# Tying each query output sum to a place in TensorE's queue

## The chip, the cores and the metric

The kernel runs on one core of a Trainium2 chip. The metric is the device time of one execution, in microseconds (us). The kernel before has a median of 917.51 us over three runs (915.57 to 920.6).

## The reference, cut to what matters

Three stages follow one another. A linear attention (4 batches, 8 heads, 576 tokens, head size 64) maps q and k through `phi`; a gated MLP, called moe1 here, works on the 2304 tokens; a top-1 mixture of 8 experts, called moe2, works on its output.

```
phi(x): p = x @ w_phi; p -= max|p|; concat(exp(p), exp(-p))
kv = phi(k)^T @ v;  z = sum(phi(k))
attn = (phi(q) @ kv) / (phi(q) @ z + 1e-6)
moe1 = (silu(xn @ w_gate) * (xn @ w_val)) @ w_out      # xn = rmsnorm(attn)
moe2 = gate * (relu(moe1[e] @ w1[e]) @ w2[e])          # e = argmax of the logits
```

## The kernel before, in words

Matmuls take their operands as pairs of 16-bit parts (high and low), so most products are three matmuls.

**Attention of batch b.** `k_unit(h)` (L275 on) projects the keys of a head and takes their exponentials; `kv(h)` (L306 on) sums them with v. `q_unit(p, rp)` (L324 on) does the same for the queries of a pair of heads, `rp` being the first or second half of the 512 main tokens, and ends in a DMA transpose issued from SP (L365), which writes the tile eT. `oo(p, rp)` (L378 on) is the query output sum of the change: 24 matmuls of eT with kv (L387) into a tile of tag ko, and a division on VectorE (`divide`, L371 on: L374, L375, L376). `oo_tail(j)` (L400 on, matmuls at L411) is the same for the last 64 tokens, twice per batch. `norm` and `ntr` (L417 on) then scale the rows and transpose them by DMA (L435) into xT of a token group.

**moe1 of token group g** (256 tokens). `m1_mm` (L509 on, matmuls at L520) makes gate and value products from xT into the PSUM tile gv: 12 matmuls for each of the two, 24 for each of 12 columns c. `m1_act` makes hT from them, and `m1_out_mm` (L535 on, matmuls at L542) sums po, six steps of 12 per group. Group 2b holds the first half of batch b, 2b+1 the second half, group 8 all the tails.

**Order.** `_weave` calls the steps of a main list in turn and after each of them so many steps of a side list that both end together. Main list of batch b: first the 24 gv steps of group 2b, with the six po steps of group 2b-1 put in behind column 1, then the same for group 2b+1. Side list of the first: the query units and output sums of the second half of batch b, its tails, and 65% of the key steps of batch b+1. Side list of the second: the rest of the keys and the first half of the queries of batch b+1. In batch 0 keys and first-half queries come ahead of all moe1 products. So an output sum of the second half is written behind the first products of group 2b, which read the xT that the first half feeds.

The order written is a priority. The framework plans all engines in a simulated timeline and lets an instruction go ahead of others that are written earlier where those aren't ready yet in its plan; the resulting order per engine is fixed in the program, and on the chip each engine works through its queue in that order.

**Shared slots.** The tag ko has two PSUM slots, which kv, oo, the tails (oot) and the router's logits (lgp, L568) take in turn. The tag E4 has four SBUF slots for the exponentials of keys and queries and for two of three eT tiles. The sums of kv lie in eight buffers that the last reader, the tail, sets free for the next batch.

Of the kernel before, what the change touches and what calls it, by code (L numbers as in the profile page):

```python
# [62 lines left out]
def body(ctx, tc, k0, kt0, q0, qt0, kk, kkt, qq, qqt, vv, vvt, w_phi, w_gv, w_out, rms_g, mid, w_g2, mbias,  # L63
         w1, w2, consts, out):
    nc = tc.nc
    V, A, G, SP, PE = nc.vector, nc.scalar, nc.gpsimd, nc.sync, nc.tensor
# [71 lines left out]
    wo = mw.tile([128, 12, 2, DM], F16, name="wo")  # L138
# [62 lines left out]
    state = {}  # L201

    def xT_group(g):
        if g not in xT:
            if g == 8:
                xT[g] = mx.tile([128, 8, 256], F16, tag="xTt", bufs=1, name="xTt")
            else:
                xT[g] = mx.tile([128, 8, 256], F16, tag="xT", bufs=3, name=f"xT{g}")
        return xT[g]
# [7 lines left out]
    def attention(b, banks, eng, pp_lo):  # L217
# [4 lines left out]
        t, m, kvs, x = {}, {}, {}, {}  # L222
# [223 lines left out]
        def seq(*fs):  # L446
            def run():
                for f in fs:
                    f()
            return run  # L450

        def L(f, *a):
            return lambda: f(*a)


        ks = [begin, seq(L(prep, "k", 4), L(prep, "k", 0), L(load, "k", 1)), L(prep, "v", 4)]
        order = [8] + list(range(8))
        for n, h in enumerate(order + [None]):
            pre = []
            if h is not None and h < 8:  # L460
                p = h // 2
# [15 lines left out]
        def q_steps(rp):  # L477
            st = []
            for p in range(5):
                fs = []  # L480
                if p < 4:
                    fs.append(L(q_unit, p, rp))
                    if rp == 0:
                        if p + 1 < 4:
                            fs.append(L(prep, "q", p + 1))
                        if p + 2 < 4:
                            fs.append(L(load, "q", p + 2))
                    elif p == 0:
                        fs.append(L(load, "q", 4))
                    elif p == 1:  # L490
                        fs.append(L(prep, "q", 4))
                if p < 4:
                    st.append(seq(*fs))
                elif rp == 1:
                    st += [L(q_unit, 4, 0)]
                if p >= 2:
                    st.append(L(oo, p - 2, rp))
            if rp == 1:
                st.append(tail_m)
            st.append(L(oo, 3, rp))  # L500
            st += [seq(L(norm, 2 * rp)), seq(L(norm, 2 * rp + 1), L(ntr, 2 * rp)), L(ntr, 2 * rp + 1)]
            return st
        tail = [L(oo_tail, 0), L(oo_tail, 1), L(norm, 4), L(ntr, 4)]
        return ks, q_steps(0), q_steps(1), tail


    hT = {}

    def m1_mm(g, c, which):  # L509
        x = xT_group(g)  # L510
        if which == 0:
            hT[g, c] = None
            state["gv", g, c] = ps_gv.tile([128, 2, 256], F32, tag="gv", name="gv")
        p = state["gv", g, c]
        f = slice(128 * c, 128 * c + 128)
        w = wgv[which]
        n = 0
        for kc in range(4):
            for wl, xl in ((0, 0), (0, 1), (1, 0)):
                PE.matmul(p[:, which, :], lhsT=w[:, kc, wl, f], rhs=x[:, 4 * xl + kc, :],  # L520
                          start=(n == 0), stop=(n == 11))
                n += 1

    def m1_act(g, c):
# [10 lines left out]
    def m1_out_mm(g, i, third):  # L535
        if third == 0:
            state["o", g, i] = ps_o.tile([128, DM], F32, tag="po", name="po")
        p = state["o", g, i]
        tk = slice(128 * i, 128 * i + 128)
        for c in range(4 * third, 4 * third + 4):  # L540
            for hl, wl in ((0, 0), (0, 1), (1, 0)):
                PE.matmul(p, lhsT=hT[g, c][:, hl, tk], rhs=wo[:, c, wl, :],  # L542
                          start=(c == 0 and hl == 0 and wl == 0), stop=(c == 11 and hl == 1))

    def m1_evict(g, i):
        p = state.pop(("o", g, i))
# [27 lines left out]
    def out_steps(g):  # L574
        st = []
        for i in range(2):
            for th in range(3):
                def s(i=i, th=th):
                    m1_out_mm(g, i, th)
                    if th == 2:  # L580
                        m1_evict(g, i)
                    if th == 0 and i == 1:
                        m1_store(g, 0)
                st.append(s)
        return st

    def group_steps(g, prev):

        st = []
        for c in range(12):  # L590
            st.append(lambda c=c: m1_mm(g, c, 0))

            def s(c=c):
                m1_mm(g, c, 1)
                m1_act(g, c)
                if prev is not None:
                    if c == 2:
                        m1_store(prev, 1)
                    if c == 4:
                        m1_logits(prev, 0)  # L600
                    if c == 6:
                        m1_logits(prev, 1)
            st.append(s)
            if c == 1 and prev is not None:
                st += out_steps(prev)
        return st
# [441 lines left out]
    narrow = ((ps_pj, "pj"),)  # L1048
    bk = list(wide)
    att = [attention(b, bk if b == 0 else narrow, EXP_SPLIT[b].split(), PREP_LO[b]) for b in range(4)]  # L1050
    done = [0]

# [20 lines left out]
    for b in range(4):  # L1073
# [8 lines left out]
        n = KSPLIT * len(ks) // 100  # L1082
        s0, s1 = side + ks[:n], ks[n:] + att[b + 1][1]
        if b == 0:
            w = []
# [6 lines left out]
        n = len(wst) // 2  # L1092
# [7 lines left out]
    rp = ctx.enter_context(tc.tile_pool(name="rp", bufs=1, side="right", reuse_waits="tile"))  # L1100
# [6 lines left out]
    n = len(w2s) * M7 // (M7 + 12)  # L1107
# [103 lines left out]
```

## Time and profile before

| | |
|---|---|
| median of three runs | 917.51 us |
| profiled execution, its own time | 921.32 us |
| its span, first to last instruction | 919.5 us |
| TensorE busy | 810.0 us (88%) |
| VectorE busy | 593.0 us (64%) |
| ScalarE busy | 431.0 us (47%) |
| granted TensorE clock, mean | 0.94 |
| mean DMA rate | 215 GB/s |

A row of the timeline is: start, duration, engine, line, operation, out<-in, shape, count, and in brackets how long the engine stood idle before it and what ended that. A matmul's row overlaps the next by some 0.2 us, since matmuls are pipelined.

### The profile page before, as it was taken

The numbers are of one execution on the slowest core, as the hardware profiler recorded it, in microseconds if no ns is written. First come the engines' busy times: TensorE is split into PE (matmuls) and PEld (weight loads), VectorE is DVE, ScalarE is ACT, GpSimd is POOL, SyncE is SP. The second block draws the span as 40 slices with busy tenths as digits, with TensorE's granted clock in tenths as the row PEclk, the third lists the DMA queues.
The fourth block names the chain that finished last, engine by engine and source line by source line (L and its number), as shares of the span: only waits on it lengthen the run. The fifth ranks groups of instructions, "written<-read, shape, count | busy, mean of one in ns | idle before, by whom it ended". The sixth has DMA issues, their size and how long they took to land. (4 is left out here: it accounts for less than half of the span.)

```text
span 919.5 us, 18449 instructions
## 1 busy us (share of the span) xinstructions
PE 810.0 (88%) x6840; PEld 557.5 (61%) x6840; DVE 593.0 (64%) x1448; ACT 431.0 (47%) x1125; POOL 86.3 (9%) x104
## 2 busy tenths in 40 slices
PE   5744699998889988979998989998899998999995
PEld 4534588776577766666786667675674443444442
DVE  6989897897688877868988866356835311221121
ACT  4787555486656666757767744234321111111110
POOL 0001030000130000211000202000010222111010
PEclk8657689999989999999999999999999999999999
DMA  8579878589899799899879986897995599699732
GB/s 278 139 193 215 209 155 191 150 215 228 212 218 260 237 242 242 212 227 242 220 213 235 234 230 189 326 344 249 266 353 132 120 224 226 143 286 257 155 70 52
DMA packets 266590, 197.39 MB, mean 215 GB/s; under 512 B 212863, under 2 KB 214271, under 8 KB 262912
## 3 DMA queue, kind: packets, MB, share of 16 engines
q1 hardware_dynamic: 263296, 186.21, 78.9%
q0 software_dynamic: 3200, 9.97, 3.4%
q8 instruction: 55, 0.90, 0.4%
q14 instruction: 39, 0.32, 0.1%
HBM read 164.92 MB, written 43.52 MB: 227 GB/s over the span
## 5 line engine op out<-in xcount | busy, mean ns | idle before, releaser
L520 PEld LDWEIGHTS <-wgv 128*128 128x128 f16 x2592 | 256.9, 100 | 69.1 <-issue 21.9
L520 PE MATMUL gv<-xT,wgv 128*128 128x256 f16 x2304 | 280.0, 280 | 20.0 <-DVE hu L530 13.2
L542 PE MATMUL po<-wo,hT 128*128 128x512 f16 x648 | 151.6, 379 | 0.1
L635 ACT ACTIVATE w2b<-w2a 128x512 f16<-128x512 f32 x128 | 80.9, 632 | 115.1 <-DMA w2a<-in_w_dram 109.3
L636 DVE SCALAR_TENSOR_TENSOR w2b<-w2a,w2b 128x512 f16<-128x512 f32 x128 | 89.7, 701 | 65.4 <-ACT w2b L635 64.8
L994 PE MATMUL m2y<-L,hsT 128*128 128x512 f16 x480 | 106.7, 379 | 4.8 <-DMA hsT<-hs 4.8
L981 ACT ACTIVATE hs<-m2h 128x512 f16<-128x512 f32 x40 | 23.9, 597 | 181.4 <-PE m2h L978 179.4
L978 PE MATMUL m2h<-L,xT 128*128 128x512 f16 x480 | 107.0, 379 | 2.0 <-DMA L<-ws 1.8
L542 PEld LDWEIGHTS <-hT 128*128 128x128 f16 x648 | 61.1, 98 | 62.0 <-DVE hT L152 1.3
L994 PEld LDWEIGHTS <-hsT 128*128 128x128 f16 x480 | 46.7, 98 | 62.0 <-DMA hsT<-hs 6.3
L978 PEld LDWEIGHTS <-xT 128*128 128x128 f16 x480 | 46.6, 98 | 58.6 <-issue 2.5
L982 DVE SCALAR_TENSOR_TENSOR hs<-m2h,hs 128x512 f16<-128x512 f32 x40 | 27.6, 691 | 80.9 <-ACT hs L981 76.5
L423 POOL TENSOR_TENSOR x<-x,g_bc 128x512 f32<-128x512 f32 x16 | 21.9, 1368 | 483.0 <-ACT xg L422 482.4
L387 PE MATMUL oo<-kv,eT 128*128 128x65 f16 x768 | 32.4, 202 | 37.3 <-DMA eT<-eq 30.6
L151 ACT CAST hT<-hu 128x256 f16<-128x256 f32 x108 | 43.5, 405 | 30.2 <-DVE hu L530 28.7
L528 DVE SCALAR_TENSOR_TENSOR th<-th,gv 128x256 f32<-128x256 f32 x108 | 44.7, 414 | 20.1 <-ACT th L527 19.7
L358 ACT ACTIVATE e<-pj,b 128x128 f32<-128x128 f32 x144 | 54.6, 379 | 4.2 <-DVE eq L152 2.5
L387 PEld LDWEIGHTS <-eT 128*128 128x128 f16 x768 | 29.6, 103 | 43.7 <-DMA eT<-eq 36.0
L359 ACT ACTIVATE e<-pj,b 128x128 f32<-128x128 f32 x144 | 55.4, 385 | 0.0
L527 ACT ACTIVATE th<-gv 128x256 f32<-128x256 f32 x108 | 41.3, 382 | 30.1 <-PE gv L520 30.0
L152 DVE TENSOR_TENSOR eq<-e,eq 128x512 f16<-128x512 f32 x72 | 52.0, 726 | 3.7 <-ACT eq L151 3.4
L997 DVE TENSOR_SCALAR y<-m2y,iBg 128x512 f32<-128x512 f32 x16 | 12.0, 751 | 65.1 <-PE m2y L994 65.1
(226 smaller groups left out, 1095.5 us busy)
## 6 DMA issues: line engine op xcount, KB each, us to landing
L<-ws SPq DMA_DIRECT2D x88, 1024.0 KB
w2a<-in_w_dram SPq DMA_DIRECT2D x128, 256.0 KB
ws<-w2b SPq DMA_DIRECT2D x128, 256.0 KB
wst<-in_w_gv_dram SPq DMA_DIRECT2D x24, 512.0 KB
wst<-in_w_out_dram SPq DMA_DIRECT2D x12, 512.0 KB
xs<-x SPq DMA_DIRECT2D x18, 256.0 KB
v<-in_vv_dram SPq DMA_DIRECT2D x16, 260.0 KB
k<-in_kk_dram SPq DMA_DIRECT2D x12, 256.0 KB
```

Of the source, the lines that this page charges most:

```text
L151: A.copy(dst_hi, src)
L152: (V if lo == "v" else G).tensor_tensor(out=dst_lo, in0=src, in1=dst_hi, op=ALU.subtract)
L358: A.activation(out=e[:, r, 0, :], in_=pp[:, j, :], func=AF.Exp, scale=sc, bias=b1[:, j:j + 1])
L359: A.activation(out=e[:, r, 1, :], in_=pp[:, j, :], func=AF.Exp, scale=-sc, bias=b2[:, j:j + 1])
L387: PE.matmul(acc[:, j, :], lhsT=et[:, hl * 8 + j * 2 + s, :], rhs=kvs[2 * p + j % 2][:, vl, s, :], start=(n == 0), stop=(n == 5))
L520: PE.matmul(p[:, which, :], lhsT=w[:, kc, wl, f], rhs=x[:, 4 * xl + kc, :], start=(n == 0), stop=(n == 11))
L528: V.scalar_tensor_tensor(out=t, in0=t, scalar=1.0, in1=p[:, 0, :], op0=ALU.add, op1=ALU.mult)
L542: PE.matmul(p, lhsT=hT[g, c][:, hl, tk], rhs=wo[:, c, wl, :], start=(c == 0 and hl == 0 and wl == 0), stop=(c == 11 and hl == 1))
L635: A.activation(out=o[:, :, 0, :], in_=t, func=AF.Copy, scale=WS)
L636: V.scalar_tensor_tensor(out=o[:, :, 1, :], in0=t, scalar=WS, in1=o[:, :, 0, :], op0=ALU.mult, op1=ALU.subtract)
L978: PE.matmul(p, lhsT=x[:, 4 * xl + kc, :], rhs=w[:, kc, half, wl, :], start=(n == 0), stop=(n == 11))
L994: PE.matmul(p, lhsT=t[:, 4 * hl + i, :], rhs=w[:, fc, wl, :], start=(fc == 0 and hl == 0 and wl == 0), stop=(fc == 7 and hl == 1))
```

## The change

`late` wraps a call. When a moe1 product has been emitted already, everything that the call puts on TensorE gets an ordering edge to the product emitted last: its place in the queue must be behind that product. It is an edge of order alone, without a semaphore. All calls of `oo` and `oo_tail` are wrapped; `m1_mm` and `m1_out_mm` record their matmuls in `state["main"]`. The first four output sums of batch 0 are emitted ahead of every moe1 product and stay free.

```
+        def late(f, *a):
+            def run():
+                if "main" in state:
+                    with tc.issue_after(state["main"].ins):
+                        f(*a)
+                else:
+                    f(*a)
+            return run
...
                 if p >= 2:
-                    st.append(L(oo, p - 2, rp))
+                    st.append(late(oo, p - 2, rp))
             if rp == 1:
                 st.append(tail_m)
-            st.append(L(oo, 3, rp))
+            st.append(late(oo, 3, rp))
...
-        tail = [L(oo_tail, 0), L(oo_tail, 1), L(norm, 4), L(ntr, 4)]
+        tail = [late(oo_tail, 0), late(oo_tail, 1), L(norm, 4), L(ntr, 4)]
...
-                PE.matmul(p[:, which, :], lhsT=w[:, kc, wl, f], rhs=x[:, 4 * xl + kc, :],
+                state["main"] = PE.matmul(p[:, which, :], lhsT=w[:, kc, wl, f], rhs=x[:, 4 * xl + kc, :],
...
-                PE.matmul(p, lhsT=hT[g, c][:, hl, tk], rhs=wo[:, c, wl, :],
+                state["main"] = PE.matmul(p, lhsT=hT[g, c][:, hl, tk], rhs=wo[:, c, wl, :],
```

## Rows read from the trace of the kernel before

**Rows 1.** Busy time by stretch: window, length, engines (count), clock, DMA share, GB/s.

```profile
313.70:375.50 61.80, 54.93 (x578) 42.92 (x578) 45.92 (x113) 38.38 (x107) 0.00 (x0) 0.97 0.92 233
...
566.50:919.50 353.00, 328.04 (x1903) 179.18 (x1903) 125.06 (x369) 66.23 (x136) 42.11 (x43) 0.99 0.77 212
```

**Rows 2.** Waits of TensorE: total us, times, longest us.

```profile
PE oo L387 <- DMA eT<-eq: 30.6, 12, 6.9
...
PE gv L520 <- DMA xT<-xg: 6.6, 4, 4.5
PE oo L387 <- DVE x L376: 5.7, 3, 3.0
```

**Rows 3.** Timeline of TensorE, 60 to 150 us: the start of batch 0's products.

```profile
84.97 0.96 PE L387 MATMUL oo<-kv,eT 128*128 128x65 f16 x24 [2.62 <-DMA eT<-eq]
...
91.08 1.50 PE L387 MATMUL oo<-kv,eT 128*128 128x65 f16 x24 [2.96 <-DMA eT<-eq]
...
96.24 1.50 PE L387 MATMUL oo<-kv,eT 128*128 128x65 f16 x24 [0.87 <-DMA eT<-eq]
102.22 7.33 PE L520 MATMUL gv<-xT,wgv 128*128 128x256 f16 x48 [4.48 <-DMA xT<-xg]
109.38 0.90 PE L387 MATMUL oo<-kv,eT 128*128 128x65 f16 x24
...
123.10 2.78 PE L520 MATMUL gv<-xT,wgv 128*128 128x256 f16 x24 [1.66 <-DVE hu L530]
125.72 2.77 PE L318 MATMUL kv<-v,ek 128*128 128x65 f32 x20
```

**Rows 4.** Timeline of TensorE, 212 to 273 us: the change from group 1 to 2.

```profile
212.98 5.40 PE L520 MATMUL gv<-xT,wgv 128*128 128x256 f16 x48
...
222.32 0.45 PE L568 MATMUL lgp<-wg,x2T 128*128 128x8 f16 x12
222.63 0.89 PE L387 MATMUL oo<-kv,eT 128*128 128x65 f16 x24
...
235.69 0.89 PE L387 MATMUL oo<-kv,eT 128*128 128x65 f16 x24 [0.57 <-DVE x L376]
...
243.56 1.63 PE L387 MATMUL oo<-kv,eT 128*128 128x65 f16 x48
...
251.45 0.89 PE L387 MATMUL oo<-kv,eT 128*128 128x65 f16 x24 [2.99 <-DVE x L376]
255.10 1.53 PE L411 MATMUL oot<-kv,eT 128*64 128x65 f16 x24 [2.76 <-DMA eT<-eq]
257.02 6.74 PE L520 MATMUL gv<-xT,wgv 128*128 128x256 f16 x48 [0.39 <-DMA xT<-xg]
263.69 0.95 PE L411 MATMUL oot<-kv,eT 128*64 128x65 f16 x24
...
272.40 1.40 PE L318 MATMUL kv<-vs,ek 128*128 128x65 f16 x30
```

**Rows 5.** Timeline of SP's DMA issues, 170 to 265 us.

```profile
192.68 2.02 SPq L365 DMA_TRANSPOSE eT<-eq  x1
...
250.07 1.49 SPq L365 DMA_TRANSPOSE eT<-eq  x1
251.65 3.48 SPq L435 DMA_TRANSPOSE xT<-xg  x2
```

**Rows 6.** Timeline of VectorE, 232 to 266 us: the ends of divisions.

```profile
242.01 0.74 DVE L376 TENSOR_TENSOR x<-oo,ep 128x256 f32<-128x256 f32 x2
...
258.14 0.41 DVE L376 TENSOR_TENSOR x32t<-oot,ep 64x256 f32<-64x256 f32 x1
```

**Rows 7.** Timeline of TensorE in batches 2 and 3.

```profile
384.03 0.90 PE L387 MATMUL oo<-kv,eT 128*128 128x65 f16 x24
...
387.82 5.40 PE L520 MATMUL gv<-xT,wgv 128*128 128x256 f16 x48 [0.87 <-DMA xT<-xg]
...
545.45 0.34 PE L387 MATMUL oo<-kv,eT 128*128 128x65 f16 x6 [2.17 <-DVE x L376]
```

More of the change, by code (lines that the diff above doesn't have):

```diff
@@ L519, in m1_mm @@
             for wl, xl in ((0, 0), (0, 1), (1, 0)):
-                PE.matmul(p[:, which, :], lhsT=w[:, kc, wl, f], rhs=x[:, 4 * xl + kc, :],
-                          start=(n == 0), stop=(n == 11))
+                state["main"] = PE.matmul(p[:, which, :], lhsT=w[:, kc, wl, f], rhs=x[:, 4 * xl + kc, :],
+                                          start=(n == 0), stop=(n == 11))
                 n += 1
@@ L541, in m1_out_mm @@
             for hl, wl in ((0, 0), (0, 1), (1, 0)):
-                PE.matmul(p, lhsT=hT[g, c][:, hl, tk], rhs=wo[:, c, wl, :],
-                          start=(c == 0 and hl == 0 and wl == 0), stop=(c == 11 and hl == 1))
+                state["main"] = PE.matmul(p, lhsT=hT[g, c][:, hl, tk], rhs=wo[:, c, wl, :],
+                                          start=(c == 0 and hl == 0 and wl == 0), stop=(c == 11 and hl == 1))
     def m1_evict(g, i):
```

## The prediction, made before the result was known

> **What bounds the kernel now.** I read the busy time by stretch first. From 566.5 us to the end TensorE works 328 of 353 us [rows 1]: whatever the attention loses or wins before that arrives at the end one for one, unless a slack behind it takes it up. Ahead of that the rows show an engine that is nearly full but not quite: 54.9 of 61.8 us in the stretch of group 3 [rows 1]. So I ask what TensorE waits for there. The list of waits says that the largest single one is output sums waiting for the transposed exponentials, 30.6 us in 12 waits; next to it stand 6.6 us of moe1 waiting for its own transposed input, and 5.7 us of output sums waiting for a division to set a ko slot free [rows 2]. A change that moves output sums back in the queue seems made for the 30.6 us. Whether it is depends on what stands behind each waiting sum, so the third view is the timeline.
>
> It shows where second-half sums stand today. In batch 0 three of them run at 84.97, 91.08 and 96.24 us, and only at 102.22 does the first moe1 product start, and it has waited 4.48 us itself, for xT [rows 3]. In batch 1 four second-half sums and the first tail run between 235.69 and 256.6, and the first product of group 2 starts at 257.02 after a wait of 0.39 us for xT [rows 4]. In both places the sums wait, but what is queued behind them could not have run either: xT wasn't there. The waits look like stalls and are the time till xT lands, partly filled with sums. By the order in which steps are written these are the sums that the edges move, since they are written behind the first products of group 2b and run ahead of them.
>
> **What the edges move.** Of 40 output groups 4 in batch 0 stay free. Of the other 36, going through the timeline with the lists that `_weave` pairs, 23 stand behind their product already. Thirteen don't: six in batch 0, three in batch 1 (the first second-half sum, tied behind the 48 products of columns 0 and 1 of group 2, and the two tails, tied behind 96 and 108), one in batch 2 and three in batch 3. In batch 1 more follow than are tied. The ko slots are taken in the order written: the sum at 222.63 had its eT transposed by an issue at 192.68, thirty us earlier, and starts directly behind the logits at 222.32, which are written ahead of it [rows 4, 5]. So three more sums, at 243.56 (two) and 251.45, go behind 257.02 with the one at 235.69.
>
> **Price of the parts**, against the profiled execution's 921.32 us, which is 3.8 above the median; the difference is then put on the median of 917.5.
>
> Edges themselves: order alone, no semaphore and no instruction, 0.
>
> Batch 0. Three sums go behind 102.22. A sum at full clock is 0.90 us, at 109.38 [rows 3], so 2.7 us of work go from a stretch in which TensorE has nothing else to one that is dense. 1.66 us of that are hidden in the wait at 123.10 for VectorE [rows 3]; without that cover it is 2.7. The waits of 2.62, 2.96 and 0.87 us go, but what is late next is xT, and the wait at 102.22 grows by as much. The last sum and the tails shift inside the dense part at no cost in TensorE's time. Cost +1.0. Bounds: +2.7 if nothing is covered; on the other side -2.96, the wait at 91.08, if the query and key units queued behind it come forward and the next batch's chain with them.
>
> Batch 1. Behind 257.02 go 0.89 + 1.63 + 0.89 for the four sums and 0.95 for a tail [rows 4], 4.4 us. The waits of 0.57, 2.99 and 2.76 us are given up for a longer wait for xT. Part is won back: on SP's queue the transpose of the tails' eT, issued at 250.07 for 1.49 us, stands right ahead of the two xT transposes at 251.65 [rows 5]. That eT needs one of four E4 slots, which the delayed sums still hold, so it will be issued after 264, and xT moves up by about 1.5 us. Cost +2.9. Bounds: -0.6, if the xT landing moves up by all of the 5.0 us from 250.07 to the start of the tail at 255.10; above, the next batch's chain. That chain is what is queued behind the delayed sums: ko slots pass through four sums, two tails and two logits before the first kv of batch 2 at 272.40 [rows 4], and kv's buffers wait for the tails. A slot is held from a sum's start to the end of its division: from 235.69 to 242.75, 7.1 us, at worst, and 3.5 us (255.10 to 258.55) at best [rows 4, 6]. Three rounds of two from 263.8 end at 285 or 274. So the first kv is between 2 and 13 us late. I take the fast end, as delayed sums are by then the oldest work in the plan, and charge none of the 2 us, since kv stands in a stretch where products can run in its place.
>
> Batch 2. One sum, at 384.03, goes behind 387.82, where a wait of 0.87 us for xT remains [rows 7]: +0.9, bounds 0 and +0.9. Its eT is a slot of E4 held 9 us longer, but the next sum runs only after the same products today.
>
> Batch 3. The sum at 545.45, which waits 2.17 us for a slot [rows 7], gets twelve products ahead of it; the two tails move a few us inside dense work. 0, bounds -2.2 and +0.9 (a sum's length). What they feed, groups 7 and 8, comes later.
>
> Sum: 1.0 + 2.9 + 0.9 + 0 = +4.8 us, 926.1 for the profiled execution, and 922 on the median.
>
> **The clock.** The 48 first products took 7.33 us at 102.22 and 6.74 at 257.02, both after waits, where 48 at 212.98 took 5.40 in dense work and 48 at 387.82 took 5.40 behind a wait of 0.87 [rows 3, 4, 7]. The same sum takes 1.50 at 96.24 and 0.90 at 109.38 [rows 3], so TensorE ran at the lower of its two levels, 1.2 of 2.4 GHz, ahead of 102.22 and came up after it. The sums that go away are part of what TensorE does ahead of them. If all 48 ran at the lower level they would take 10.8 us, 3.5 and 4.1 us more than now. I put none of it into the sum, as both stretches already begin cold, and carry it as a rival. The Trainium skill, in "TensorE: Matmul & The Clock Gate", section "HAM oscillation — how this bites in real kernels", holds that an engine left idle between bursts drops to half rate and starts the next burst there; that speaks against this change. By that rule the sum would be 7.6 us higher, and the two cold starts of the trace agree with it in direction.
>
> **Rivals.**
>
> *Faster, through the chain.* The delayed work of the second half leaves VectorE, ScalarE and SP free just when the first half's rows are normed and transposed. xT of group 2 lands up to 5.0 us sooner [rows 5], and in batch 0 the units behind 91.08 up to 2.96 [rows 3], while the moved sums are taken up by waits that come anyway (6.9 us stand idle in the stretch of group 3 [rows 1]). For it: the first products of groups 0, 2 and 4 all wait for xT. Against it: the gain must exceed 4.4 us of sums in batch 1, or the sums must be hidden. It decides from an xT landing of about 252.6 on. Time: 917.5 - 5.0 - 3.0 = 909.5.
>
> *Long lag.* Slots turn over at the slow rate, the first kv of batch 2 starts near 285 instead of 272.4, and group 4's xT is late by as much: 12.7 + 1.0 + 0.9 = +14.6, 932. For it: the 7.1 us row. Against it: key units of batch 2 don't wait for ko and can gather it back.
>
> *The clock stays low* at both starts: +4.8 + 7.6, 930.
>
> *Nothing arrives*: the order changes, but each displaced us falls into one of the later waits for xT, or the plan reorders around the edges. Time 917.5. For it: 23 groups stand in place already and the eT waits of those stay; against it: the stretch from 257 is dense, the rows of timeline there name no idle.
>
> **How the numbers follow.** Forecast 0.42, with its own range of 917 to 927; faster 0.23; long lag 0.14; clock 0.07; nothing 0.14. A difference within 0.5% (4.6 us, 912.9 to 922.1) is about what a measurement can't tell from no change. The forecast lies on that edge and gives half of its chance to either side. Faster 0.23; same 0.14 + 0.21 = 0.35; slower 0.21 + 0.14 + 0.07 = 0.42. The range of 8 in 10 takes in both ends: 908, a little under the faster case, to 932, the long lag.
>
> **What would show it.** In the profile of the changed kernel the first product of group 2 stands ahead of all second-half sums of batch 1, behind one wait for xT of 5 us or more in place of 0.39. The list of waits has eT waits of about 24 us (30.6 less 2.62, 2.96 and 0.87), and xT waits that have grown by about as much as the eT and division waits fell. The first kv of batch 2 starts within 275 us or, by the long lag, around 285; xT transposes of group 2 are issued around 250. Wrong would be: eT waits down by 15 us or more with xT waits unchanged (then the stalls were real), the three batch 0 sums still ahead of the first product, or a first product of group 2 before 252.6.

## The result, and the profile after

The changed kernel takes 929.63 us (median of 20 runs, 922.7 to 935.86) where the kernel before, timed beside it, takes 919.62 (20 runs, 913.61 to 925.41): a ratio of 1.0103, interval 1.0078 to 1.0129. By that ratio it is slower by about 9.5 us (the medians differ by 10.0); the forecast was 4.8.

The two profiled executions are closer together than the medians. The one after took 925.72 us with a span of 923.8, which is 3.9 under its own median; the one before took 921.32 with 919.5, which is 1.7 over the median of its 20 runs. So the traces show 4.3 us in place of 9.5, and what follows from them accounts for those 4.3.

First the list of TensorE's waits after the change (total us, times, longest):

```profile
PE oo L387 <- DMA eT<-eq: 21.5, 9, 6.4
PE gv L530 <- DVE hu L540: 17.0, 14, 3.0
PE gv L530 <- DMA xT<-xg: 9.6, 3, 8.2
...
PE lgp L578 <- DMA x2T<-x: 8.3, 4, 3.8
PE oo L387 <- DVE wu L170: 4.9, 1, 4.9
```

The waits for eT fall by 9.1 us, from 30.6 [rows 2], but not all of that comes from the stalls that the change takes sums away from. The wait of 4.9 us that ends with a weight conversion on VectorE (wu) is most likely one of the same kind: it stands ahead of the second of the four free sums of batch 0, where the trace of before has a wait for eT. That sum reads no converted weight. First before, then after:

```profile
71.74 1.50 PE L387 MATMUL oo<-kv,eT 128*128 128x65 f16 x24 [5.49 <-DMA eT<-eq]
```

```profile
69.96 1.50 PE L387 MATMUL oo<-kv,eT 128*128 128x65 f16 x24 [4.92 <-DVE wu L170]
```

Counted with it, these waits fall from 30.6 to 26.4 us, while the tied sums of batch 0 lose waits of 6.45 us (2.62, 2.96 and 0.87 [rows 3]). Other waits grow: xT is waited for 3.0 us longer [rows 2], and the router's logits wait 8.3 us for their transposed input. Before, that was

```profile
PE lgp L568 <- DMA x2T<-x: 3.3, 2, 2.0
```

TensorE works 808.4 us of the span after and 810.0 before, so its idle time grew from 109.5 to 115.4.

Where? The busy times by stretch, from the start of one group to that of another (window, length, the busy time of TensorE, its weight loads, VectorE, ScalarE and GpSimd with their counts, clock, DMA share, GB/s). Before: to group 0, groups 0, 1, 2, 3, 4 and 5, the rest:

```profile
0.00:102.20 102.20, 54.60 (x528) 43.72 (x528) 89.19 (x199) 71.93 (x197) 5.74 (x10) 0.67 0.81 205
102.20:166.70 64.50, 62.83 (x558) 54.77 (x559) 54.98 (x120) 31.28 (x74) 6.95 (x9) 0.89 0.75 175
166.70:257.00 90.30, 79.91 (x788) 58.39 (x787) 72.82 (x177) 60.34 (x170) 3.99 (x6) 0.98 0.85 210
257.00:313.70 56.70, 55.70 (x608) 44.23 (x608) 50.96 (x110) 37.35 (x96) 7.74 (x9) 0.98 0.93 244
313.70:387.80 74.10, 66.25 (x660) 48.57 (x660) 56.46 (x135) 48.33 (x137) 4.80 (x6) 0.98 0.91 230
387.80:526.60 138.80, 127.39 (x1405) 98.69 (x1405) 117.76 (x280) 95.72 (x270) 10.80 (x15) 0.98 0.94 227
526.60:919.50 392.90, 363.35 (x2297) 209.15 (x2296) 150.80 (x433) 86.08 (x187) 46.27 (x49) 0.99 0.77 213
```

The same seven stretches after:

```profile
0.00:99.60 99.60, 51.77 (x456) 40.83 (x456) 87.38 (x189) 72.05 (x195) 7.83 (x10) 0.66 0.81 210
99.60:164.10 64.50, 57.00 (x586) 49.84 (x587) 57.14 (x127) 30.57 (x73) 9.37 (x9) 0.94 0.73 178
164.10:248.00 83.90, 77.33 (x673) 56.12 (x672) 66.79 (x157) 56.08 (x161) 4.61 (x6) 0.98 0.83 200
248.00:318.70 70.70, 61.45 (x674) 47.75 (x672) 53.99 (x117) 39.82 (x96) 6.40 (x9) 0.98 0.91 235
318.70:390.50 71.80, 67.92 (x722) 50.89 (x719) 60.88 (x147) 50.00 (x141) 4.98 (x6) 0.98 0.93 243
390.50:531.50 141.00, 127.83 (x1399) 98.14 (x1399) 117.48 (x275) 93.37 (x265) 12.70 (x15) 0.98 0.90 219
531.50:923.80 392.30, 365.12 (x2338) 210.29 (x2338) 152.64 (x441) 89.95 (x200) 46.09 (x49) 0.98 0.77 212
```

The lengths differ by -2.6, 0, -6.4, +14.0, -2.3, +2.2 and -0.6, together +4.3. Groups 0 to 2 start earlier, by 2.6, 2.6 and 9.0 us; then group 2 takes 14 us more, 5.75 of them TensorE's work and 8.25 idle, and group 3 starts 5.0 late. That difference stays to the end within a few us. The 5.75 us are in the main a balance: four sums (4.44 us) and one more tail (0.95) come into the stretch, and so do 26 matmuls of po (5.23), while 87 matmuls of kv (4.63) leave it. Work moves over the borders of stretches, so idle time tells more than length. It grows by 5.8 us in group 0 and by 8.25 in group 2, into which tied sums go, and falls by 3.8 in group 1 and by 4.0 in group 3.

The timeline of TensorE after, at the start of batch 0's products (start, duration, engine, line, operation, and in brackets the idle time and what ended it):

```profile
99.64 4.69 PE L530 MATMUL gv<-xT,wgv 128*128 128x256 f16 x24 [8.21 <-DMA xT<-xg]
104.16 0.90 PE L387 MATMUL oo<-kv,eT 128*128 128x65 f16 x24
104.90 2.78 PE L530 MATMUL gv<-xT,wgv 128*128 128x256 f16 x24
107.52 0.90 PE L387 MATMUL oo<-kv,eT 128*128 128x65 f16 x24
...
112.00 0.90 PE L387 MATMUL oo<-kv,eT 128*128 128x65 f16 x24
```

The three sums of [rows 3] now stand behind the first product, and the one wait ahead of it is 8.21 us in place of 4.48. And around group 2; left out are keys, queries, po, logits and products without a wait:

```profile
245.38 5.40 PE L530 MATMUL gv<-xT,wgv 128*128 128x256 f16 x48
...
255.78 1.64 PE L387 MATMUL oo<-kv,eT 128*128 128x65 f16 x48
...
264.47 2.80 PE L387 MATMUL oo<-kv,eT 128*128 128x65 f16 x48 [2.94 <-DVE x L376]
267.08 4.46 PE L530 MATMUL gv<-xT,wgv 128*128 128x256 f16 x38
271.48 0.95 PE L411 MATMUL oot<-kv,eT 128*64 128x65 f16 x24
...
275.72 1.47 PE L530 MATMUL gv<-xT,wgv 128*128 128x256 f16 x12 [3.02 <-DVE hu L540]
277.12 0.95 PE L411 MATMUL oot<-kv,eT 128*64 128x65 f16 x24
...
285.64 2.78 PE L530 MATMUL gv<-xT,wgv 128*128 128x256 f16 x24 [1.43 <-DVE hu L540]
...
289.74 2.78 PE L530 MATMUL gv<-xT,wgv 128*128 128x256 f16 x24 [1.04 <-DVE hu L540]
...
300.44 1.40 PE L318 MATMUL kv<-vs,ek 128*128 128x65 f16 x30
```

The 48 products at 245.38 are the last column of group 1 and the first of group 2, with no wait between them: xT of group 2 has landed by then. The four sums and two tails of [rows 4] follow inside group 2. The waits 2.94, 3.02, 1.43 and 1.04 add up to 8.4 of the stretch's 9.25 us of idle time (before it had 1.0). The longest can be followed further. The instruction hu that ends it (th and hu are steps of `m1_act`) stands behind th on ScalarE, and ScalarE had been idle for 3.34 us till a piece of moe2's weights was loaded (w2a), whose conversion (w2b) and two pieces of norm stand ahead of th in its queue:

```profile
272.64 0.63 ACT L645 ACTIVATE w2b<-w2a 128x512 f16<-128x512 f32 x1 [3.34 <-DMA w2a<-in_w_dram]
...
274.40 0.36 ACT L537 ACTIVATE th<-gv 128x256 f32<-128x256 f32 x1
```

```profile
275.25 0.42 DVE L540 SCALAR_TENSOR_TENSOR hu<-th,gv 128x256 f32<-128x256 f32 x1
```

In group 2's stretch ScalarE waits longer for such loads, and VectorE for ScalarE's part of the conversion. First before, then after:

```profile
ACT w2b L635 <- DMA w2a<-in_w_dram: 12.7, 12, 2.6
DVE w2b L636 <- ACT w2b L635: 3.2, 4, 1.5
```

```profile
ACT w2b L645 <- DMA w2a<-in_w_dram: 21.1, 17, 3.3
DVE w2b L646 <- ACT w2b L645: 12.0, 11, 2.4
```

No run moves a conversion, so this is a candidate for the added idle time and not its shown cause. The first kv of batch 2 starts at 300.44, 28 us later than at 272.40 [rows 4]. SP's queue after:

```profile
239.43 2.62 SPq L435 DMA_TRANSPOSE xT<-xg  x2
...
262.69 2.36 SPq L365 DMA_TRANSPOSE eT<-eq  x1
```

The transposes of xT go out at 239.43, 12.2 us ahead of 251.65 [rows 5], and the tails' eT behind them at 262.69 instead of 250.07. What xT follows is not the tails' eT but the normed rows of the first half (xg), whose last piece VectorE writes at 251.96 before and at 240.06 after:

```profile
251.22 0.74 DVE L427 SCALAR_TENSOR_TENSOR xg<-x,ss,xg 128x512 f16<-128x512 f32 x1
```

```profile
238.65 1.41 DVE L427 SCALAR_TENSOR_TENSOR xg<-x,ss,xg 128x512 f16<-128x512 f32 x2 [1.83 <-ACT xg L426]
```

### The profile page after: what moved, and what is told of

Same layout as the page of the kernel before. It is cut to its first block, busy times and chain, and to the rows that moved or that the text cites. A ratio compares the mean times of both kernels' runs of the same rounds, so it can differ in the third digit from the quotient of the medians.

```text
span 923.8 us, 18459 instructions
## 1 busy us (share of the span) xinstructions
PE 808.4 (88%) x6840; PEld 553.8 (60%) x6840; DVE 596.3 (65%) x1448; ACT 431.8 (47%) x1125; POOL 92.0 (10%) x104
## 5 line engine op out<-in xcount | busy, mean ns | idle before, releaser
L530 PEld LDWEIGHTS <-wgv 128*128 128x128 f16 x2592 | 254.2, 100 | 70.7 <-issue 19.9
L552 PE MATMUL po<-wo,hT 128*128 128x512 f16 x648 | 154.0, 384 | 3.5 <-DVE x L560 1.8
L358 ACT ACTIVATE e<-pj,b 128x128 f32<-128x128 f32 x144 | 55.8, 387 | 5.2 <-DVE eq L152 2.5
L359 ACT ACTIVATE e<-pj,b 128x128 f32<-128x128 f32 x144 | 56.6, 393 | 0.0
L152 DVE TENSOR_TENSOR hT<-hu,hT 128x256 f16<-128x256 f32 x108 | 47.7, 441 | 10.1 <-ACT hT L151 10.0
L318 PE MATMUL kv<-vs,ek 128*128 128x65 f16 (+1 forms) x720 | 42.8, 206 | 12.2 <-DVE ek L152 9.3
```

Of the source, the lines that this page charges most:

```text
L152: (V if lo == "v" else G).tensor_tensor(out=dst_lo, in0=src, in1=dst_hi, op=ALU.subtract)
L318: PE.matmul(acc[:, s, :], lhsT=l, rhs=r_, start=(n == 0), stop=(n == len(ops) - 1))
L358: A.activation(out=e[:, r, 0, :], in_=pp[:, j, :], func=AF.Exp, scale=sc, bias=b1[:, j:j + 1])
L359: A.activation(out=e[:, r, 1, :], in_=pp[:, j, :], func=AF.Exp, scale=-sc, bias=b2[:, j:j + 1])
L530: state["main"] = PE.matmul(p[:, which, :], lhsT=w[:, kc, wl, f], rhs=x[:, 4 * xl + kc, :], start=(n == 0), stop=(n == 11))
L552: state["main"] = PE.matmul(p, lhsT=hT[g, c][:, hl, tk], rhs=wo[:, c, wl, :], start=(c == 0 and hl == 0 and wl == 0), stop=(c == 11 and hl ...
```

## The experiments

Four theories were on record. **A**: the ties cost at the start of a group, where sums were cover, and by the keys' chain behind them that shares the ko slots. **B**: the loss arises in batch 0 and is handed on. **C**: an edge that moves a sum makes the framework plan everything behind it anew; the loss is the other order's, and does not add up from parts. **F**: the moved sums' own time on TensorE.

**One batch at a time** (N = 0, 1, 2, 3):

```
-                if "main" in state:
+                if "main" in state and b == N:
```

> The edges on batch 0's output sums and tails alone; all others free as before. Theory A (each tie at the start of group 2b costs there, and the costs add up to the 9 to 10 us of the whole change): +1 to +3 us, first kv of batch 1 a few us after 125.7. Theory B (the loss begins in batch 0, whose later tails push the first kv of batch 1 from 125.7 to 133.2, and is handed on from batch to batch): +6 to +10 us by itself. Theory C (any edge makes the framework plan another order for everything behind it, and the loss is that order's, not the moved sums'): a shift of either sign that does not fit the sum.

> The edges on batch 1 alone. Theory A: the largest single share, +4 to +7 us; the trace up to 190 us is that of before, the four second-half sums stand behind the first products of group 2, TensorE idles 5 us or more between 257 and 313 where it idled 1 before, and the first kv of batch 2 comes 10 us or more after 272.4. Theory B: +0 to +2 us, since batch 0 is untouched. Theory C: either sign.

> The edges on batch 2 alone, where one sum is moved behind its product and the other five stand behind theirs already. Theory A: +0 to +2 us. Theory B: 0. Theory C: a shift of either sign, as large as that of the batches in which more is moved.

> The edges on batch 3 alone, where one sum and two tails are moved by 4 to 6 us inside dense work and nothing of the attention follows. Theory A: -1 to +1 us. Theory B: 0. Theory C: either sign, small, since little is left to plan.

Beside 920.25 us of before, batch 0 alone takes 934.42 (ratio 1.0159, interval 1.0117 to 1.0201), batch 1 alone 930.7 (1.0125, 1.0076 to 1.0174), batch 2 alone 931.61 (1.0133, 1.0091 to 1.0175) and batch 3 alone 917.95 (0.9979, 0.9948 to 1.001). The differences, 14.2, 10.5, 11.4 and -2.3, add up to 33.8 us; all ties together cost 10.0 by the same measure. So B falls (batches 1 and 2 lose without batch 0), and A and F in the additive form do too; A's ranges are missed in batches 0 to 2. Batch 2 is the clearest: a single sum of 0.9 us moves behind group 4's first products. Its trace by stretch, groups 4 and 5 and the rest:

```profile
385.40:530.10 144.70, 126.67 (x1429) 97.83 (x1429) 117.24 (x280) 95.77 (x271) 11.39 (x15) 0.99 0.88 211
530.10:927.80 397.70, 366.06 (x2292) 210.04 (x2292) 149.35 (x432) 85.40 (x184) 46.16 (x49) 0.98 0.78 213
```

Groups 4 and 5 take 5.9 us more than the 138.80 of before with 0.7 less work in them, so it is idle time; and the rest, in which no sum is tied, takes 4.8 more than 392.90, of which 2.7 are more time for TensorE's work there. Up to the tie the two kernels have one program, and the 2.4 us between their starts of group 4 (385.40 and 387.80) are what one execution differs from another. Behind it the two programs differ widely: at least 555 of TensorE's matmuls, 250 instructions of VectorE, 136 of ScalarE and 60 DMA issues of SP stand in another order.

In batch 1 alone the forecast's picture holds, one long wait for xT ahead of group 2 instead of 0.39 [rows 4]:

```profile
254.19 4.06 PE L530 MATMUL gv<-xT,wgv 128*128 128x256 f16 x19 [10.81 <-DMA xT<-xg]
```

Even so the price is larger than the 2.9 us that it forecast. In the stretches of groups 1 and 2 of this run, TensorE idles 14.2 and 4.4 us where it idled 10.4 and 1.0 before, 7.2 us more:

```profile
164.70:254.19 89.49, 75.27 (x668) 53.94 (x668) 73.05 (x168) 60.07 (x168) 3.99 (x6) 0.96 0.86 214
254.19:312.06 57.87, 53.50 (x646) 43.96 (x646) 46.39 (x106) 32.96 (x81) 6.52 (x9) 0.97 0.89 234
```

**Tails alone, sums alone.** For the one the sums, for the other the tails are left untied:

```
-                    st.append(late(oo, p - 2, rp))
+                    st.append(L(oo, p - 2, rp))
...
-        tail = [late(oo_tail, 0), late(oo_tail, 1), L(norm, 4), L(ntr, 4)]
+        tail = [L(oo_tail, 0), L(oo_tail, 1), L(norm, 4), L(ntr, 4)]
```

> Edges on the two tails of each batch alone; the sums of the main tokens are free as before. Theory A (the loss is a late chain: the first kv of the next batch takes its ko slot behind the delayed sums, tails and logits, and what isn't gathered back arrives at the next xT): the tails stand right ahead of the logits and kv in the slot order, so tying them alone keeps a good part, +4 to +8 us, with the first kv of batch 2 at 280 or later. Theory F (the loss is the sums' own time on TensorE, moved from a stretch without other work to a dense one, about 0.9 us each): one tail in batch 1 alone is moved across the start of a group, so +0 to +2 us.

> Edges on the 32 output sums of the main tokens alone; the tails are free. The tails still follow the sums in the ko order. Theory A: +5 to +9 us, a little under the whole change, first kv of batch 2 between 275 and 295. Theory F: nine of the ten moved pieces remain, +6 to +9 us, but with the first kv of batch 2 no more than 5 us late.

Tails alone: 927.53 us (1.0063, 1.0029 to 1.0098); sums alone: 931.47 (1.0111, 1.0072 to 1.0149). Beside 920.45 of before these are 7.1 and 11.0 us, 18.1 together, where all ties cost 10.0: again no sum of parts. The sums alone cost as much as the whole change. Tails alone lie in A's range, and the first kv of batch 2 comes at 290.41, as A had it; sums alone lie above both ranges by their median, though not by their interval.

**The ko slots without the logits.** If the late kv comes from ko's turns and costs the time, taking the logits out of the turns must help the changed kernel:

```
-        p = ps_ko.tile([128, NE], F32, tag="ko", name="lgp")
+        p = ps_o.tile([128, NE], F32, tag="po", name="lgp")
```

> The whole change, with the router's logits (lgp) in the slots of tag po in place of ko; nothing else differs. The logits of group 2b-1 then no longer stand between the tails and the first kv of the next batch. Theory A: the first kv of batch 2 comes forward from 300 to 285 or before, and the time falls by 3 to 8 us against the whole change (+2 to +7 over the kernel before). Theory F: the sums still stand where they stood, +8 to +11 us over the kernel before.

> The kernel before, with the logits in the slots of tag po: the control for the other. Theory A: little stands to be won, since the logits run 4 to 8 us ahead of the first kv of batch 2 already (264.6 and 269.0 against 272.4): -4 to +1 us. Theory F: -1 to +1 us.

Changed kernel with it: 932.89 us (1.0116, 1.0074 to 1.0159); before with it: 921.11 (0.9989, 0.9961 to 1.0018, beside 920.45). The changed kernel lies 12.4 us over 920.45, so it does not gain as A had it; F's range, 8 to 11, lies within the interval. The first batch 2 kv of the two, the changed one first:

```profile
300.37 1.40 PE L318 MATMUL kv<-vs,ek 128*128 128x65 f16 x30
```

```profile
290.25 0.23 PE L318 MATMUL kv<-vs,ek 128*128 128x65 f16 x2
```

In the changed kernel kv starts where it did, so the logits' turns are not what delays it. In the one without ties kv is 18 us later than at 272.40 [rows 4] and in sum nothing is lost: a late first kv is not in itself the price. That part of A falls. The same run shows that a long group 2 is not in itself the price either. Without any tie that group takes 72.15 us, 8.3 of them idle, more than the changed kernel's 70.70:

```profile
235.79:307.94 72.15, 63.81 (x645) 47.76 (x646) 51.76 (x111) 37.93 (x93) 6.45 (x9) 0.95 0.89 224
```

Its program differs from that of before in the order of at least 1425 matmuls, and it is as fast: another order need not cost.

**Another plan without a tie.** What is left is C, and its test is to move the plan by something that ties nothing: the share of the next batch's key steps that is written beside the even groups, 55% or 75% in place of 65%, without and with the ties:

```
-KSPLIT = 65
+KSPLIT = 55        # or 75
```

> The kernel before with 55% instead of 65% of the next batch's key steps beside groups 2b (11 of 21 steps instead of 13); no sum is tied. The theory of a plan (the ties cost because the framework lays out everything behind them anew, and the order written was fitted to the plan of before) says: another plan without any tie loses too, 3 to 12 us, 923 to 932. The theory of a local price (the moved sums and the waits next to them cost the time) says nothing is moved behind a product here: within 2 us of before, 918 to 922.

> The kernel before with 75% of the next batch's key steps beside groups 2b (15 of 21 instead of 13); no sum is tied. Theory of a plan: 3 to 12 us over before, 923 to 932. Theory of a local price: 918 to 922.

> The changed kernel with 55% of the key steps beside groups 2b. Theory of a plan: the excess over the untied kernel of the same split isn't the 9.5 us of the split of 65%; it comes out anywhere from -5 to +15 us, by the plan. Theory of a local price: the same sums stand behind the same products, so the excess over the untied kernel of the same split is again 7 to 12 us.

> The changed kernel with 75% of the key steps beside groups 2b: the keys of the next batch, which came 34 us late in the changed kernel (first key unit of batch 2 at 287 instead of 253 us), are written two steps further forward. Theory of a plan: the excess over the untied kernel of the same split is anywhere from -5 to +15 us; if the late keys are what costs, it is at the low end and the time falls under 925. Theory of a local price: 7 to 12 us over the untied kernel of the same split.

| key steps beside groups 2b | no ties: us, ratio to before | ties: us, ratio to before | ties cost (medians) |
|---|---|---|---|
| 55% | 937.1, 1.0162 (1.0129 to 1.0195) | 929.72, 1.0079 (1.005 to 1.0109) | -7.4 |
| 65% | 919.62, 1 | 929.63, 1.0103 (1.0078 to 1.0129) | +10.0 |
| 75% | 925.86, 1.0061 (1.0034 to 1.0088) | 935.83, 1.0148 (1.0125 to 1.0172) | +10.0 |

Without any tie the time moves by 5.4 and by 16.7 us; the second is more than C allowed. So a plan that moves nothing behind a product can cost more than the change itself, and C's mechanism is there and large enough. The splits do move key steps, though, and what the moved steps themselves cost isn't parted from what the other plan costs. The excess of the ties is less clear: +10.0 at 75% is what the local theory forecast (C allowed it as well), -7.4 at 55% is not, and by the medians it lies under C's lower end of -5 too. At all three splits the tied program has the same order in every queue with the ties on first-half sums and without them, so -7.4 belongs to the second half's sums and the tails alone. What remains against a price that belongs to the moved sums are the parts: batch 0 alone costs 14.2 us, and the other batches' ties, of which those of batches 1 and 2 alone cost 10.5 and 11.4, bring that down to 10.0 when they join it. The guess on record that the late keys are what costs, and that the 75% split brings them back to under 925, falls: 935.83.

At 55% the traces show where the ties pay. The stretches of groups 2 and 3 without ties, and then with them:

```profile
249.30:316.60 67.30, 60.75 (x614) 46.23 (x614) 50.44 (x114) 40.92 (x105) 5.97 (x9) 0.95 0.94 238
316.60:400.20 83.60, 69.82 (x794) 52.61 (x791) 71.51 (x173) 59.72 (x174) 4.62 (x6) 0.98 0.96 234
```

```profile
248.00:315.80 67.80, 61.29 (x695) 48.10 (x696) 55.92 (x125) 41.59 (x108) 6.86 (x9) 0.97 0.96 246
315.80:389.60 73.80, 68.03 (x703) 50.60 (x702) 61.55 (x148) 51.66 (x148) 4.49 (x6) 0.98 0.91 233
```

Group 2, into which batch 1's sums go, takes the same in both (67.30 and 67.80), where at 65% it went from 56.70 to 70.70: at 55% it is long without ties. (At 55% two of the four sums are behind group 2's start without ties already.) The ties win 9.8 us in group 3, whose idle time falls from 13.8 to 5.8 us. Two second-half sums of batch 2 stand in it without ties, at 387.53 and 393.07, and leave it with them; that is 1.8 us of work, and neither has a wait ahead of it, so the 8.0 us of idle time are lost elsewhere in the plan. None of these versions beats the kernel before: the two below its time, batch 3 alone and the logits out of ko (the latter by its ratio alone), lie within their intervals.

What stays open: by which slot or engine the other plan loses, and how much of the loss is its share and how much the sums'. In group 0 a local share is likely: its idle time grows with the ties from 1.7 to 7.5 us, with batch 0's alone to 5.8, and at 55% from 1.5 to 4.9. Group 2's 14.0 us are no measure of one, as the untied runs at 55% and with the logits out of ko show. In group 2 the added idle time is ended by divisions and by hu on VectorE, but VectorE works a smaller share there, 53.99 of 70.70 us after and 50.96 of 56.70 before; that points to the order of the queues, its own and ScalarE's, and not to its load. Which instruction would have to move was not tried. Nor was a longer list of E4 slots, for which there is no room in SBUF. The difference between 4.3 us in the traces and 9.5 in the medians is open as well, as timed runs leave no trace.

## Why the prediction was right in sign and half of the size

*Which sums move.* Right. The three of batch 0 stand behind 99.64, and batch 1's four sums and two tails, the untied followers among them, behind the first products of group 2.

*The stalls were cover, and eT's waits come back elsewhere.* Right in the main: 26.4 us of waits for eT are left, with the one put down to wu, where about 24 was forecast. That they would come back as waits for xT holds for group 0, whose wait grew from 4.48 to 8.21 us. In all, xT took 3.0 us more and the logits 5.0; the waits for divisions fell from 5.7 [rows 2] to 2.9 in place of growing. The mark of real stalls, eT's waits down by 15 us or more with xT's unchanged, did not occur.

*Batch 0, +1.0.* By group 1's start the changed kernel is 2.6 us ahead. The first xT lands 2.6 us sooner, within the forecast's lower bound of -2.96, and the sums run at 0.90 us behind the product where two took 1.50 ahead of it [rows 3]. The stretch of group 0 has the same length, with 57.00 us of work for 62.83 and the rest idle: 5.8 us of idle time that the forecast did not have, which cancel the work saved there.

*Batch 1, +2.9: the failed term.* The step "xT moves up by about 1.5 us" was wrong in size: it took SP's queue with the tails' eT for what held xT back, but xT goes out when the first half's rows are normed. The transposes went out 12.2 us sooner, and group 2 began 9.0 us sooner, past the point of 252.6 from which the forecast let the faster case win. By the forecast's own mark that is wrong. The faster case did not win, because the forecast put at nothing what follows the moved sums: "charge none of the 2 us, since kv stands in a stretch where products can run in its place". The moved sums and tail, 4.4 us in the forecast, measure 5.4 in group 2. kv did leave the stretch, but TensorE idles 8.25 us more there, in waits that divisions and hu end. Gain and loss leave 5.0 us at group 3's start, where the terms for batches 0 and 1 gave 3.9: two errors that nearly cancel, which is luck.

*The next batch's chain.* kv of batch 2 was forecast 2 to 13 us late and was 28. Its price by the long-lag rival was its lateness, 12.7 us at group 4. Group 4 started 2.7 us late, and the logits experiment shows 18 us of lateness at no cost in sum. The rival's time of 932 is nearer to the median of 929.63 than the forecast's 922; its mechanism did not occur.

*Batches 2 and 3, +0.9 and 0.* In the whole change groups 4 and 5 take 2.2 us more, the rest 0.6 less. But alone batch 2 costs 11.4. The forecast treated each batch's ties as a price to be added, which is the assumption that the runs refute.

*The clock.* The rival's 7.6 us do not show. After the longer wait the first 48 products of group 0 took 4.69 + 2.78 = 7.47 us beside 7.33 [rows 3], and over the group the granted clock rose from 0.89 to 0.94. At group 2 the 48 products of 245.38 took 5.40 at a granted clock of 1.00, with no wait ahead of them, where those of 257.02 took 6.74 [rows 4] at 0.79. But two of the moved sums, at 264.47 behind a wait of 2.94, ran at 0.50 and took 2.80 us where two took 1.64 at 255.78: 1.2 us of the lower level that the forecast had at the products and not here. The Trainium skill's rule, in "TensorE: Matmul & The Clock Gate", section "HAM oscillation — how this bites in real kernels", that the burst after an idle stretch starts at half rate, agrees with 4.69 for 24 products against 2.78; but in batch 0 the work that ran at that rate before was also the sums, and moving them put them behind the rise.

*The faster rival* had the right direction: group 2 starts 9.0 us earlier and group 0 2.6. It lacked the idle time in both groups. *Nothing arrives* is excluded by the interval.

## What to carry to other kernels

In a program whose order a framework plans, an ordering edge is not a local edit: it can redraw every queue behind it, and what it costs depends on the rest of the plan, here -7 to +10 us for the same lines of code. Before an order is judged by an edit, measure how far the time moves under edits that have nothing to do with the idea, such as another split of a list; a change of 1% inside that spread says little of its own idea. And compare idle time by stretch, since work that moves over a border changes lengths without a cost. And when a wait is to be removed, look at what the sums or products beside it cover: an instruction moved out of a stall needs a place where something else is waiting.

## What the runs showed of the hardware

The same 6840 matmul records took TensorE between 808.2 us at a mean granted clock of 0.946 (tails alone) and 816.8 at 0.932 (the changed kernel at 75%), so the time of the same work alone can set two profiled executions 8 us apart. One program repeats within some 13 us: 913.61 to 925.41 before, 922.7 to 935.86 after. What follows a wait of some 3 us ran at either level of the clock: after the change two sums behind a wait of 2.94 us had a granted clock of 0.50 (1.2 of 2.4 GHz) and took 2.80 us, where the two at 255.78 took 1.64 at 1.00; the 12 products behind the wait of 3.02 at 275.72 had 1.00.
